# Result stores of two batches in their own stream, wider idle matmuls, a stacked short tile, and another order

## The chip, the core and the metric

The kernel runs on one core of a Trainium2 chip. A core has a matrix engine (PE, with its weight loads PEld), three engines for elementwise work (DVE, ACT and POOL) and SP, which only issues DMA transfers, in order. All engines take their instructions in program order and wait for each other through semaphores. The metric is the device time of one execution in microseconds (us); lower is better.

## The reference

The inputs are q, k and v (8 batches, 8 heads, 576 positions, 64 channels a head) and four weights. For each batch:

```
q_d, k_d, v_d = means over groups of 4 positions (576 -> 144)
pooled        = repeat(softmax(q_d k_d^T / 8) v_d, 4)
local         = softmax over |i - j| < 4 of (q k^T / 8), times v
x             = pooled + local, as [576, 512]
u             = x + (relu(x^T w_tok1) w_tok2)^T       # tokens: 576 -> 256 -> 576
out           = u + relu(u w_ch1) w_ch2               # channels: 512 -> 1536 -> 512
```

## The kernel before

Everything is written by one Python function that places instructions by hand. Each piece of work is a generator that yields steps (engine, planned duration, what must have been made, PSUM or SBUF slots taken and given back) and emits its instructions after each step. `drive` simulates clocks for all engines and always emits the step that can begin first; steps within `PATIENCE` of the first, on the same engine, go by the order of the list of streams, which for the first part of the kernel is the string `PRIORITY` (one letter for a group of streams). So the planned durations and that string set the order of every engine's instructions, and of the DMAs in SP's queue; on the chip only semaphores and program order count.

- *Attention, batch by batch.* `load` fetches q and k (tile qk), `load_v` fetches v in pieces (vr) which POOL adds to the pooled values vd, `load_w` fetches v in the order of the local windows (vw). `pooled` makes the scores sd of a pair of heads (PE), their exponentials pd, the transposed td, the product ad, and od (DVE, L551); after the last pair two DMAs copy od into rows of vw (L557). `local` makes the scores sc of a tile of 128 positions (the fifth tile has 64), masks, softmax (DVE and ACT, tile P), the transposed pT and the product av, which takes the pooled result along with vw; ACT copies it to x. The local products of a batch thus wait for vw and for od's copy.
- *Exponentials.* In batches listed in `BIASED` the maximum goes into four ACT activations as a bias (L515, reading PSUM); in the others DVE subtracts it (L521) and ACT runs one activation (L524).
- *Token mix (`mix`).* Batch 0 uses float32 weights. From batch 1 on, weights and x are split in a high and a low part (`token_split`; `splits`: xh, ACT copies, DVE subtracts) and `mm3` runs three passes over them, `PASSES` = high by high, high by low, low by high. u is the sum; its maximum scales it to two float16 parts, uh.
- *Channel mix.* Batches 0 and 1 run plain products: `first` (12 tiles by uh and the weight C1, matmuls c, L128) and `second` (by C2); `second_up` adds the result to u (L891) and issues the store (L892) in the same step. Batches 2 to 7 run a product scheme with fewer multiplications, from sums of the weights that POOL and DVE make meanwhile (`weight_sums`, stored to DRAM by `stores`, L912 and L916, and fetched as units, L1010); `first_blocks` (L1029) and `second_blocks` (L1197) are its products, `after_second` adds to u, and `results` stores.
- *Weights.* They arrive as 64-bit words. `weight_loads` (L241) fetches W (token weights, nine pieces), C1 (twelve pieces of 512 KB) and `C2.loads` (L379) the twelve of C2; ACT, POOL and DVE turn each into float32 (`to_f32`, L220, L223, L225). `in_turn` makes each of these transfers wait for the third one before it (`DEPTH`), and SP with it.
- *Idle matmuls.* Until batch 0's uh is planned, `keep_busy` (L170) fills planned gaps of PE with products of a constant tile.

The first batches' work overlaps: batch 1's attention and mix lie between batch 0's channel products, batch 2's between batch 1's.

## Time and profile before

| | |
|---|---|
| median of 3 runs | 894.14 us (891.07 to 894.2) |
| profiled execution | 896.11 us, its span 894.0 us |
| mean granted PE clock | 0.981 |
| busy | PE 95%, PEld 77%, DVE 71%, ACT 47%, POOL 44% |
| DMA | 152.85 MB, mean 171 GB/s |

The span runs from the first to the last instruction. An engine's busy time is that of its instructions; matmuls are pipelined and their ends are modelled, so a busy PE can be slower than its peak, and the granted clock tells how fast it was allowed to run. Where a line names a releaser ("<-"), the instruction waited for that one last.

### The profile page before, as it was taken

How to read it: one execution, taken by the hardware profiler on the slowest of the kernel's cores; microseconds unless marked ns; L12 is line 12 of the kernel's file. 1: busy time of each engine (PE TensorE's matmuls, PEld its weight loads, DVE VectorE, ACT ScalarE, POOL GpSimd, SP SyncE). 2: the span in 40 equal slices, each digit the busy share in tenths (PEclk: the TensorE clock that was granted, in tenths of full speed). 3: DMA queues.
4: the chain of work that ended last, by engine and by line, in shares of the span. 5: the costliest groups of instructions: out<-in, count | busy, mean ns of one | idle time of the engine just before them, and what ended most of it. 6: DMA issues, size and time to landing. Idle time of an engine off the chain costs nothing.

```text
span 894.0 us, 26687 instructions
## 1 busy us (share of the span) xinstructions
PE 850.5 (95%) x11112; PEld 685.4 (77%) x11112; DVE 636.2 (71%) x1410; ACT 420.2 (47%) x978; POOL 392.4 (44%) x593
## 2 busy tenths in 40 slices
PE   7699999897999999999999999999999999999998
PEld 6566777686779877888868887888768886887776
DVE  6669998568886756868585876678485885666762
ACT  2366552134553335754365525654265535643740
POOL 6228475769496203662066403761066501420430
PEclk9798999898999999999999999999999999999999
DMA  8775524663264308636673557545574554247653
GB/s 267 262 270 188 163 64 138 221 210 91 87 230 116 92 26 292 219 111 174 192 243 135 161 184 247 200 135 172 171 241 146 154 192 133 95 125 211 196 162 121
DMA packets 71656, 152.85 MB, mean 171 GB/s; under 512 B 16560, under 2 KB 32432, under 8 KB 69488
## 3 DMA queue, kind: packets, MB, share of 16 engines
q1 hardware_dynamic: 71536, 151.16, 52.1%
q8 instruction: 87, 1.43, 0.6%
q14 instruction: 33, 0.27, 0.1%
HBM read 128.32 MB, written 20.45 MB: 166 GB/s over the span
## 4 chain that ended last, share of the span: by engine, by line
PE 81%; DVE 9%; DMA 4%; POOL 2%; ACT 2%; issue 2%; SPq 1%; ACTq 0%; DVEq 0%; POOLq 0%
PE dX L1197 12%; PE c L128 12%; PE t L128 11%; PE cx L1029 11%; PE dY L1197 6%; PE cy L1029 5%; PE ad L541 3%; PE dZ L1197 3%; PE cz L1029 3%; PE av L619 3%; PE sc L577 2%; PE sd L503 2%; PE pT L605 2%; PE td L531 2%; PE t L690 2%
## 5 line engine op out<-in xcount | busy, mean ns | idle before, releaser
L1109 POOL TENSOR_TENSOR h<-t,h 128x288 f16<-128x288 f32 x108 | 82.6, 768 | 213.4 <-ACT h L1098 211.6
L1029 PEld LDWEIGHTS <-wa 128*128 128x128 f16 x864 | 82.0, 98 | 26.7 <-issue 4.7
L1197 PEld LDWEIGHTS <-wc_S 128*128 128x128 f16 x864 | 82.8, 98 | 21.4 <-issue 1.3
L1029 PEld LDWEIGHTS <-wb 128*128 128x128 f16 x648 | 62.6, 98 | 19.6 <-issue 4.1
L128 PE MATMUL c<-uh,CW 128*128 128x288 f16 x576 | 76.7, 289 | 0.0
L128 PE MATMUL c<-h,CX 128*128 128x288 f16 x576 | 76.2, 290 | 0.1
L1197 PEld LDWEIGHTS <-wc_A 128*128 128x128 f16 x648 | 62.7, 98 | 15.5 <-issue 0.2
L128 PEld LDWEIGHTS <-CX 128*128 128x128 f16 x576 | 55.6, 99 | 15.8 <-issue 0.8
L128 PEld LDWEIGHTS <-CW 128*128 128x128 f16 x576 | 55.7, 99 | 14.7 <-issue 0.6
L1029 PE MATMUL cx<-uh_T,wb 128*128 128x288 f16 x432 | 64.7, 286 | 1.3 <-DVE y L1140 1.3
L128 PE MATMUL t<-xh,W 128*128 128x512 f32 x210 | 58.9, 414 | 7.1 <-DVE xh L660 5.0
L487 POOL TENSOR_TENSOR qd<-qk 128x144 f32<-128x144 f32 x48 | 28.8, 599 | 83.9 <-DMA qk<-in_qk_dram 83.9
L487 POOL TENSOR_TENSOR qd<-qd,qk 128x144 f32<-128x144 f32 x96 | 61.7, 642 | 6.3
L457 POOL TENSOR_TENSOR vr<-vr 72x256 f32<-72x256 f32 x48 | 36.4, 759 | 58.5 <-DMA vr<-in_vr_dram 51.2
L1197 PE MATMUL dY<-h,wc_S 128*128 128x288 f16 x432 | 58.4, 286 | 0.0
L128 PE MATMUL t<-W,hid 128*128 128x288 f32 x336 | 58.4, 309 | 0.0
L1197 PE MATMUL dX<-h,wc_S 128*128 128x288 f16 x432 | 58.2, 286 | 0.0
L1197 PE MATMUL dX<-h,wc_A 128*128 128x288 f16 x432 | 57.0, 286 | 0.0
L1098 ACT ACTIVATE h<-t 128x288 f16<-128x288 f32 x108 | 47.7, 442 | 15.6 <-DVE t L1113 15.5
L128 PEld LDWEIGHTS t<-xh,W 128*128 128x128 f32 x210 | 37.1, 188 | 17.6 <-DVE xh L660 7.6
L1244 DVE SCALAR_TENSOR_TENSOR u<-dX,io,u 128x288 f32<-128x288 f32 x48 | 24.7, 515 | 34.3 <-PE dX L1197 33.7
L128 PEld LDWEIGHTS t<-W,hid 128*128 128x128 f32 x336 | 46.6, 189 | 0.0
(206 smaller groups left out, 1946.7 us busy)
## 6 DMA issues: line engine op xcount, KB each, us to landing
qk<-in_qk_dram SPq DMA_DIRECT2D x32, 580.0 KB
wa<-d1a SPq DMA_DIRECT2D x36, 512.0 KB
wc_S<-d_S SPq DMA_DIRECT2D x48, 384.0 KB
wb<-d1b SPq DMA_DIRECT2D x36, 384.0 KB
wc_A<-d_A SPq DMA_DIRECT2D x36, 384.0 KB
vw<-in_vw_dram SPq DMA_DIRECT2D x8, 1280.0 KB
vr<-in_vr_dram SPq DMA_DIRECT2D x64, 144.0 KB
vw<-in_vw_dram SPq DMA_DIRECT2D x8, 1024.0 KB
```

The source lines that it names most:

```text
L128: nc.tensor.matmul(ps, lhs(a), rhs(c), start=first and i == 0, stop=last and i == 2, **kw)
L457: nc.gpsimd.tensor_add(t[:, 0:2], t[:, 0:2], t[:, 2:4])
L487: nc.gpsimd.tensor_add(to, to if f > 1 else x[0], x[f])
L503: nc.tensor.matmul(ps[:G, par, Sd * g:Sd * g + Sd], st.qd[p, pr, 0, G * g:G * g + G], st.qd[p, pr, 1], start=True, stop=True)
L531: nc.tensor.transpose(ps[:G, par, o:o + G], pd[:, par, g, G * kg:G * kg + G], ident[:G, :G])
L541: nc.tensor.matmul(ps[:, g, par], pt[:, par, kg, G * g:G * g + G], st.vd[:, kg, 2 * pr + par], start=kg == 0, stop=kg == 1)
L619: nc.tensor.matmul(ps[QB * j:QB * j + QB, par, D * hp:D * hp + D], pt[p, hp, QB * j:QB * j + QB], st.vw[p, g, h, D * hp:D * hp + D], start ...
L1029: nc.tensor.matmul(ps, w[:, a, 128 * k:128 * k + 128], uh[x][:, k, c], start=first_ and k == j == 0, stop=k == 1 and j == 2, skip_group_ch ...
L1098: nc.scalar.activation(here().h[:, PARTS.index(name), 0], x, f)
L1109: nc.gpsimd.tensor_tensor(h[:, i, 1], getattr(here(), x), h[:, i, 0], ALU.subtract)
L1197: nc.tensor.matmul(ps, w[:, k, a], H[k][:, i, c], start=first_ and k == j == 0, stop=k == 5 and j == 2, skip_group_check=True)
L1244: nc.vector.scalar_tensor_tensor(u, blocks_[b, o, name], io, u, ALU.mult, ALU.add)
```

## The change

- The eight result stores of batch 0, and those of batch 1, leave `second_up`; a stream of their own (`plain_results`) issues each in a step on SP, planned no earlier than `LATE` = 14 us after its data. Those of batches 2 to 6 are planned 3 us after theirs.
- `in_turn` counts bytes: a transfer waits until it and those under way before it are at most 1.2 MB.
- An idle matmul has 384 columns (the 192 read twice) instead of 192, and there are half as many for each unit of planned gap; 0.85 of a gap is filled instead of 0.6, at most 12 units instead of 8.
- The token mix's fifth tile has only 64 rows. The weight's other 64 rows now hold its low part, and x's high part is copied to both halves, so that two passes (`STACKED`) do what three did. ACT copies twice instead of once.
- `BIASED` takes in batches 0 and 1; in batch 0 the last multiply of the local softmax (L600) moves from DVE to POOL.
- vr of batch 0 lies in buffers of u instead of x, xh and od.
- Planned durations, first clocks, `PATIENCE`, `HELD`, a factor 1.04 on DVE's steps, and the string `PRIORITY` differ, so the order of instructions differs on all engines.

```diff
@@ -23,18 +23,21 @@
...
 PASSES = ((0, 0), (0, 1), (1, 0))
+STACKED = ((0, 0), (1, 1))
 FIRSTS = (0, 1, 4, 5, 8, 9)
...
 LIVE = 3
-PATIENCE = 0.15
+PATIENCE = 0.1
 GATE = (0, 0, 1, 2, 3)
-BIASED = range(2, 8)
+BIASED = range(0, 8)
 ON_POOL = range(2, 8)
+LATE = 14.0
 HOP = 0.12
-HELD = 0.6
+HELD = 0.8
+MARGIN = 1.04
 TURN = 0.1
-DEPTH = 3
-PRIORITY = "LpWUMASETaCDPHmQw"
+UNDER_WAY = 1.2e6
+PRIORITY = "SUMWpTaCEADPLHmQw"
@@ -123,9 +126,9 @@
...
-    def mm3(ps, lhs, rhs, first, last, **kw):
-        for i, (a, c) in enumerate(PASSES):
-            nc.tensor.matmul(ps, lhs(a), rhs(c), start=first and i == 0, stop=last and i == 2, **kw)
+    def mm3(ps, lhs, rhs, first, last, passes=PASSES, **kw):
+        for i, (a, c) in enumerate(passes):
+            nc.tensor.matmul(ps, lhs(a), rhs(c), start=first and i == 0, stop=last and i == len(passes) - 1, **kw)
@@ -138,14 +141,14 @@
...
-    clock = dict(A=2.0, G=5.0, V=2.0, P=0.0, S=0.0, D=0.0, R=0.0, X=0.0)
+    clock = dict(A=2.0, G=5.0, V=2.0, P=6.6, S=0.0, D=1.5, R=0.0, X=0.0)
     now = [0.0]
...
     def step(engine, us, *needs, at=None, take="", give="", mode=None, port=False):
-        return engine, us, needs, at, take.split(), give.split(), mode, port or engine == "G"
+        return engine, us * MARGIN if engine == "V" else us, needs, at, take.split(), give.split(), mode, port or engine == "G"
@@ -166,8 +169,9 @@
...
             ps = P1("busy")
-            for _ in range(8 * n // 3):
-                nc.tensor.matmul(ps[:, :192], junk[:, :128], junk, start=True, stop=True)
+            wide = junk.unsqueeze(1).to_broadcast([128, 2, 192])
+            for _ in range(4 * n // 3):
+                nc.tensor.matmul(ps[:, :384].rearrange("p (k n) -> p k n", k=2), junk[:, :128], wide, start=True, stop=True)
@@ -191,7 +195,7 @@
...
                 if ("uh", 0, 1) not in made and free["g"]:
-                    keep_busy(min(8, int((t - clock["P"]) * 0.6 / 0.22)))
+                    keep_busy(min(12, int((t - clock["P"]) * 0.85 / 0.22)))
                 mode = m
@@ -216,29 +220,33 @@
...
         lo, hi = words[:, :, 0], words[:, :, 1]
-        yield step("A", 0.1 + n * 0.0011, at=at)
+        yield step("A", 0.28 + n * 0.00077, at=at)
         nc.scalar.activation(hi.bitcast(F32), hi.bitcast(F32), AF.Prelu, scale=2.0 ** -112, alpha=-2.0 ** 32)
-        yield step("G", 0.1 + n * 0.0016)
+        yield step("G", 0.09 + n * 0.0013)
...
         nc.gpsimd.tensor_scalar(lo, lo, 2.0 ** -29, -0.501, ALU.mult, ALU.add)
-        e = yield step("V", 0.08 + n * 0.0012, *needs, port=True)
+        e = yield step("V", 0.1 + n * 0.0014, *needs, port=True)
         nc.vector.scalar_tensor_tensor(lo if y is None else y(), hi, 3, lo, ALU.logical_shift_left, ALU.bitwise_or)
...
-    def in_turn(dma):
-        if len(queue) >= DEPTH:
-            tc.add_manual_dep(dma.ins, queue[-DEPTH].ins.name, mybir.DependencyInfo(mybir.DependencyClass.Sync, mybir.DependencyReason.DATA),
-                              reason="few transfers under way")
-        queue.append(dma)
+    def in_turn(dma, nbytes):
+        before, n = len(queue), nbytes
+        while before and n + queue[before - 1][1] <= UNDER_WAY:
+            before -= 1
+            n += queue[before][1]
+        if before:
+            tc.add_manual_dep(dma.ins, queue[before - 1][0].ins.name, mybir.DependencyInfo(mybir.DependencyClass.Sync, mybir.DependencyReason.DATA),
+                              reason="few bytes under way")
+        queue.append((dma, nbytes))
...
             raws[i] = T([src.shape[0], 2 * n], U32, tag, f"{name}{i}_raw")
-            in_turn(nc.sync.dma_start(raws[i], src))
+            in_turn(nc.sync.dma_start(raws[i], src), src.shape[0] * n * 8)
             made[name, "raw", i] = fetched(src.shape[0] * n * 8, n * 0.7e3)
@@ -256,8 +264,10 @@
...
         nc.scalar.copy(f[:, 0], WY[i])
+        if f.shape[0] == short:
+            nc.scalar.copy(f[:, 1], WY[i])
         e = yield step("V", 0.08 + n * 0.0012, port=True)
-        nc.vector.tensor_tensor(f[:, 1], WY[i], f[:, 0].bitcast(F32), ALU.subtract)
+        nc.vector.tensor_tensor(W1[-1][short:, 0] if f.shape[0] == short else f[:, 1], WY[i], f[:, 0].bitcast(F32), ALU.subtract)
         make(("W", "split", i), e)
@@ -309,7 +319,7 @@
...
             nc.scalar.activation(f[:, 0], y, AF.Copy, scale=self.s[i // 4])
-            t = yield step("V", 0.75, port=True)
+            t = yield step("V", 0.88, port=True)
             nc.vector.scalar_tensor_tensor(f[:, 1], y, self.s[i // 4], f[:, 0], ALU.mult, ALU.subtract)
@@ -376,7 +386,7 @@
...
                     t = four[:, i % 4]
-                in_turn(nc.sync.dma_start(t, u32(c2[i])))
+                in_turn(nc.sync.dma_start(t, u32(c2[i])), 2 ** 19)
                 self.raws.append(t)
@@ -420,8 +430,7 @@
...
-            tag = "x" if st.b or i < 4 else "xh" if i < 7 else "od"
-            ts[i] = T([G, 4, 128], F32, tag, f"vr{st.b}_{i}")
+            ts[i] = T([G, 4, 128], F32, "x" if st.b else "u", f"vr{st.b}_{i}")
             nc.sync.dma_start(ts[i], vr[st.b, g, pr].rearrange("p (r c) -> p r c", r=4))
@@ -474,7 +483,7 @@
...
             for h in range(2):
-                yield step("V", 0.44, at=0.0 if h else st.at[hp])
+                yield step("V", 0.5, at=0.0 if h else st.at[hp])
                 o = st.qd[:, hp, 0, G * h:G * h + G].rearrange("p (r g) -> p r g", g=HG)
@@ -522,7 +531,7 @@
...
             nc.scalar.activation(pd, pd, AF.Exp, scale=0.125 / 16)
-        yield step("P", 0.55 if b < 2 else 0.46, take="gg", give="w")
+        yield step("P", 0.5 if b < 2 else 0.46, take="gg", give="w")
         ps = P2(f"td{b}_{pr}")
@@ -532,7 +541,7 @@
...
         nc.scalar.copy(pt, ps[:G, :, :2 * Sd].rearrange("p a (k w) -> p a k w", k=2))
-        yield step("P", 1.2 if b < 2 else 0.97, ("v", b, 2 * pr), ("v", b, 2 * pr + 1), *([("full", b - 1)] if b and pr == 0 else []),
+        yield step("P", 1.1 if b < 2 else 0.97, ("v", b, 2 * pr), ("v", b, 2 * pr + 1), *([("full", b - 1)] if b and pr == 0 else []),
                    *([("od", b)] if pr else []), take=one, give="w")
@@ -596,8 +605,8 @@
...
         nc.vector.reciprocal(r, r)
-        yield step("V", 0.5, at=0.0, port=True)
-        nc.vector.tensor_tensor(w, w, r.unsqueeze(2).unsqueeze(2).to_broadcast([n, H, 8, 5]), ALU.mult)
+        yield step("G" if b < 1 else "V", 0.9 if b < 1 else 0.5, at=None if b < 1 else 0.0, port=True)
+        (nc.gpsimd if b < 1 else nc.vector).tensor_tensor(w, w, r.unsqueeze(2).unsqueeze(2).to_broadcast([n, H, 8, 5]), ALU.mult)
         before = [("av", b, t - 2)] if t > 1 else [("av", b - 1, 3 + t)] if b else []
@@ -652,17 +661,21 @@
...
             for t in range(NT if b else 0):
-                yield step("A", 0.62, ("x", b, t), *([("over", 0, 0)] if b == 1 else []),
+                yield step("A", 0.62 if t < NT - 1 else 1.2, ("x", b, t), *([("over", 0, 0)] if b == 1 else []),
                            *([("t1", b, t - 3)] if t > 2 else [("mixed", b - 1)] if b > 1 else []))
                 xh = st.xh[t] = T([128, 2, 512], F32R, "xh", f"xh{b}_{t}")
-                nc.scalar.copy(xh[:, 0], xf(t))
+                if t < NT - 1:
+                    nc.scalar.copy(xh[:, 0], xf(t))
+                else:
+                    for p in (0, short):
+                        nc.scalar.copy(xh[p:p + short, 0], xf(t)[:short])
                 e = yield step("V", 0.7, port=True)
...
             for t in range(NT):
-                e = yield step("P", 1.8 if b == 0 else 1.5 if b == 1 else 1.42, *([("W", "split", t), ("xh", b, t)] if b else [("W", "y", t), ("x", 0, t)]),
+                e = yield step("P", 1.8 if b == 0 else (1.5 if b == 1 else 1.42) * (1 if t < NT - 1 else 2 / 3), *([("W", "split", t), ("xh", b, t)] if b else [("W", "y", t), ("x", 0, t)]),
                                take="" if t else f"gg>{b}")
@@ -673,7 +686,7 @@
...
                         mm3(st.acc[:, f], lambda a: W1[t][:, a, 128 * f:128 * f + 128], lambda a: st.xh[t][:, a],
-                            t == 0, t == NT - 1)
+                            t == 0, t == NT - 1, PASSES if t < NT - 1 else STACKED)
                 make(("t1", b, t), e)
@@ -889,8 +902,15 @@
...
             nc.vector.scalar_tensor_tensor(us[c], banks[c], io, us[c], ALU.mult, ALU.add)
-            nc.sync.dma_start(out[b, 128 * c:128 * c + 128, s0:s0 + N], us[c])
+            make(("into", b, ch, c), e, LATE)
         make(("over", b, ch), e)
+
+    def plain_results(b):
+        for ch in range(2):
+            for c in range(4):
+                yield step("S", 0.1, ("into", b, ch, c))
+                nc.sync.dma_start(out[b, 128 * c:128 * c + 128, HALF * ch:HALF * ch + HALF], ready[b].u[ch][c])
+                fetched(147e3, 250e3)
@@ -1222,7 +1242,7 @@
...
             for name, h in (("A12", 0), ("A22", 1)):
-                yield step("S", 0.1, ("into", b, o, name))
+                yield step("S", 0.1, ("out", b, o, name))
                 c = o + 2 * h
@@ -1243,6 +1263,7 @@
...
                 make(("into", b, o, name), e)
+                make(("out", b, o, name), e, 3.0 if b < B - 1 else 0.0)
@@ -1315,7 +1336,7 @@
...
         group["Q"] = products[2:]
-        streams = [reopen()] + [x for k in PRIORITY for x in group[k]]
+        streams = [reopen(), plain_results(0), plain_results(1)] + [x for k in PRIORITY for x in group[k]]
         late = []
```

## The prediction

> **What bounds the kernel now.** I read the page's head first, then busy time by stage, then the chain of waits in the weakest stages, then the DMA queue there.
>
> ```profile
> span 894.0 us, 26687 instructions
> PE 850.5 (95%) x11112; PEld 685.4 (77%) x11112; DVE 636.2 (71%) x1410; ACT 420.2 (47%) x978; POOL 392.4 (44%) x593
> ```
>
> The span is PE's: 43.5 us idle in all. Stages, in stretches of 20 us or more, and the bad places in 5 us (columns: span, then busy time of PE, PEld, DVE, ACT, POOL with instruction counts, granted clock, DMA share, GB/s):
>
> ```profile
> 140.00:160.00 20.00, 18.42 (x259) 14.98 (x258) 17.35 (x44) 5.43 (x10) 15.16 (x21) 1.00 0.59 212
> 400.00:500.00 100.00, 98.02 (x1274) 79.73 (x1272) 71.98 (x159) 51.42 (x125) 41.89 (x65) 1.00 0.59 187
> 600.00:700.00 100.00, 96.56 (x1237) 78.80 (x1236) 71.69 (x158) 52.09 (x126) 39.67 (x62) 1.00 0.56 183
> ...
> 165.00:170.00 5.00, 2.43 (x20) 1.70 (x18) 1.44 (x3) 0.42 (x1) 4.53 (x9) 1.00 0.69 231
> 170.00:175.00 5.00, 3.33 (x134) 2.90 (x135) 2.56 (x3) 1.91 (x4) 4.70 (x8) 0.65 0.15 49
> 175.00:180.00 5.00, 5.00 (x84) 3.50 (x83) 1.72 (x3) 2.45 (x6) 0.23 (x1) 0.66 0.33 78
> 205.00:210.00 5.00, 2.87 (x30) 2.11 (x29) 4.90 (x10) 0.96 (x2) 4.43 (x7) 1.00 0.13 39
> 210.00:215.00 5.00, 2.36 (x22) 2.17 (x23) 3.35 (x9) 4.03 (x12) 4.60 (x7) 0.75 0.48 125
> 215.00:220.00 5.00, 5.00 (x155) 4.17 (x154) 3.01 (x8) 1.00 (x3) 4.62 (x7) 0.57 0.31 82
> ```
>
> From 400 us on PE is 96 to 98% busy, so a microsecond that batches 0 and 1 give back earlier reaches the end whole: what runs there is PE work that waits for little but PE. Earlier, two holes matter: 165 to 175 (4.2 us idle) and 205 to 215 (4.8 us), and behind each of them PE runs cold: (3.33+5.00)x0.35 = 2.9 us lost at clock 0.65, and 2.36x0.25+5.00x0.43 = 2.7 us at 0.75 and 0.57. Together 14.6 us. The chain says where the first comes from (start, duration, what):
>
> ```profile
> 137.09 0.53 DVE u L891
> 137.63 0.37 SPq L892
> 138.11 2.50 DMA vr<-in_vr_dram
> ...
> 153.20 0.53 DVE u L891
> 154.18 0.61 SPq L466
> 154.84 11.42 DMA vw<-in_vw_dram
> 166.70 0.73 SPq L557
> 167.48 3.35 DMA vw<-od
> 170.87 1.81 PE av L619 x111
> ```
>
> Twice the chain leaves a result (u, L891) for a load of batch 1 that has nothing to do with it: the store (L892) stands in SP's queue ahead of vr (values to be pooled) and of vw (attention's values), and SP issues in order. SP's waits from 116 to 182 us and POOL's from 100 on (total, times, longest), and three instructions of DVE and PE that date what follows:
>
> ```profile
> SPq L892 <- DVE u L891: 18.0, 2, 16.3
> SPq L912 <- DVE S L955: 7.8, 2, 6.8
> ...
> POOL vr L439 <- DMA vr<-in_vr_dram: 10.5, 2, 10.2
> ...
> 113.91 1.48 DVE L225 SCALAR_TENSOR_TENSOR CY<-C_raws 128x512 uint32<-128x512 uint32 x1
> 156.10 0.42 DVE L551 TENSOR_TENSOR od<-ad,rd 72x256 f32<-72x256 f32 x1
> 213.73 0.61 DVE L764 SCALAR_TENSOR_TENSOR uh<-u,us,uh 128x288 f16<-128x288 f32 x1 [0.98 <-ACT uh L762]
> ...
> 205.09 1.64 PE L128 MATMUL c<-h,CX 128*128 128x288 f16 x12
> ```
>
> SP stood 16.3 us (to 137.6) with vr behind the store, and POOL stood idle 10.2 us for that vr. The last pooled result of batch 1 (od) is ready at 156.5, but its copy into vw (L557) goes out at 166.70, when vw itself has landed. Batch 0's last product ends at 206.7, batch 1's first input (uh) is ready at 214.3: the second hole.
>
> **The change, part by part.**
>
> *Stores of batches 0 and 1 in a stream of their own, planned 14 us after their data.* Same eight DMAs for each batch, moved behind later loads in SP's queue. vw may load once C2's raws are read (the last CY conversion ends at 115.4), so it is issued near 121, where the store began to block, instead of 154 and lands in 11.4 us (its row), by 133. The copy of od then waits for od alone: 157 instead of 166.7, and PE's av starts at about 160 instead of 170.1; earlier still if vr, no longer behind the store, lets POOL finish vd ten microseconds sooner. The first hole goes whole, 4.2+2.9 = 7.1. In the second PE is out of work. Batch 1's mix starts 10 us earlier, but batch 0's products also end 7 us earlier, so I give back only half: 3.8 of 4.8+2.7. Late next there: DVE, which gives batch 1's attention and its splits. Sum of this part **-10.9**; bounds -14.6 and 0. A store that is late holds a u buffer, but batch 2 takes batch 0's and batch 3 batch 1's only with the results of their own mix, which stand well over 14 us behind the last use. Cost 0; if it were wrong, up to 14 once for each.
>
> By the Trainium skill ("TensorE: Matmul & The Clock Gate", the section on HAM oscillation) the clock falls to half after idle gaps of more than about 3.4 us. The trace departs from it here: 3.33 us of work in the five from 170, and 2.43 in the five before, were followed by 0.66 with PE fully busy. Were the 2.9 us not this hole's, the sum would come out at 883 instead of 880; I go by the rows.
>
> *Stacked short tile.* In batches 1 to 7 the last tile of the first token product goes from three passes to two: 2 matmuls of 128x512 fewer for each batch. Price by the chain, where they stand back to back, and what is added:
>
> ```profile
> 340.31 2.79 PE t L128 x12
> ...
> L658 ACT CAST xh<-x_last x7: 602/607/622, 184.6 to 767.6; 128x512 fp32r<-128x512 f32 x7
> ...
> PE t L128 <- DVE xh L660: 4.6, 4, 1.9
> ```
>
> 0.2325 each, x14 = **-3.3**. Added: a second ACT copy of 0.61 us ahead of the same tile's split, seven times. ACT is 47% busy over the span, but PE already waits for splits, 4.6 us from 400 on; if each of the seven came late by the whole copy it would cost 4.3. The planner counts the copy (1.2 for 0.62) and puts PE's tile behind other products, so I take 0 and keep +4.3 as a bound.
>
> *Idle matmuls.* Half as many of twice the columns: about the same time for each unit, but planned for 0.85 of a gap instead of 0.6, at most 12 units instead of 8.
>
> ```profile
> 44.88 5.52 PE t L672 x8
> 54.07 3.63 PE t L672 x8
> ```
>
> The same eight products of batch 0's token mix run cold the first time, 5.52 against 3.63, behind the wait for od's copy that the next part shows: 1.9 us to be had if the filler bridged it. But the planner, which places the filler, does not see that wait. A filler that overruns costs at most its extra length, a fourth more than now on some 2 us. Taken 0; +1 to -1.9.
>
> *Bytes instead of transfers under way (1.2 MB for three).* For W four go at once; for C1 and C2 (524 KB) two instead of three. SP's queue in the first 40 us, the pooled result, and how C1's second half landed:
>
> ```profile
> 32.38 5.66 SPq L241 DMA_DIRECT2D W_raw<-in_w_dram  x4
> 38.09 1.53 SPq L557 DMA_DIRECT2D vw<-od  x2
> 32.66 0.42 DVE L551 TENSOR_TENSOR od<-ad,rd 72x256 f32<-72x256 f32 x1
> ...
> 47.04 4.01 SPq L241 DMA_DIRECT2D C_raw<-in_c_dram  x4
> 50.82 0.65 POOL L223 TENSOR_SCALAR C_raw<-C_raw 128x512 uint32<-128x512 uint32 x1 [8.58 <-DMA C_raw<-in_c_dram]
> 54.32 0.78 POOL L223 TENSOR_SCALAR C_raw<-C_raw 128x512 uint32<-128x512 uint32 x1 [0.27 <-DMA C_raw<-in_c_dram]
> ```
>
> Batch 0's od is ready at 33.1 and waits 5 us behind four W loads, each held by the rule of three. Under the new rule the last of them waits for the last C1 load and not for the first W of the four: about 1 us earlier; 5 if the new order puts od's copy ahead. Against it: C1's first lands after 3.8 us (47.0 to 50.8), the third at 54.3, so one every 1.75 us with three under way; a load's round trip is then 3x1.75 = 5.3 us. Two under way make one every 1.9 us if the round trip falls back to 3.8, and every 2.6 if it stays: an estimate from these rows, 0.15 to 0.9 us later for each of C1's twelve loads, whose sums are on the way to the first product. I take the lower end, since the loads queue behind each other now; it about cancels the 1 us: **0**, from -5 to +10.5.
>
> *Bias in the activation for batches 0 and 1, and one multiply of batch 0 on POOL.*
>
> ```profile
> L521 DVE TENSOR_TENSOR pd<-sd,mxd x16: 443/448/454, 11.6 to 143.3; 72x288 f32<-72x288 f32 x16
> L515 ACT ACTIVATE pd<-sd,mxd x96: 361/372/382, 210.6 to 715.2; 72x144 f32<-72x144 f32 x96
> ```
>
> DVE loses 16x0.448 = 7.2 us and gains 8 scalings of four columns; ACT issues 32 activations of 0.372, 11.9 us, where it issued 8 of four times the columns, hidden by its 53% idle; POOL, 44% busy, takes five multiplies of about the size of L521's, which DVE is rid of. In batch 0 the pooled result comes 2 to 3 us sooner, but is held by the W loads above; in batch 1 it is part of what lets av start at 160. Counted there; by itself 0, to -3.
>
> *The rest.* Stores of batches 2 to 6 three microseconds later: 0. What stands behind them in SP's queue are weight loads that PE does not wait for in the rows above. vr of batch 0 in u buffers: both it and the first u come before any of them is wanted twice, 0. Planner durations, margin, held share, patience, first clocks and the priority string alter the order everywhere: no row prices that. The nearest is how two like stretches differ, 98.0 against 96.6 busy: 1.5 us in 100. Taken 0; six stretches make -6 to +9.
>
> Sum: 10.9+3.3 = 14.2. The profiled execution took 896.1 (2.1 around its span), 2.0 above the median of 894.1; the terms are differences, so I set them against the median: **880**. Own range of this case 872 to 888.
>
> **The rivals.**
> - *Little of the holes closes:* batch 1's attention is DVE's (17.35 of 20 busy at 140 to 160), so mix 1 comes hardly earlier and the second hole grows by what the first gives. For: that DVE row. Against: DVE is busy only 5.7 of the 15 us from 165 on. With a fourth of the 14.6: 894.1-3.3-3.6 = 887.
> - *The change doesn't do what it says:* something else holds vw's load in SP's queue; stores of weight sums (L912) wait there too. Then 894.1-3.3 = 891. Against: their two waits on DVE took 7.8 us, the result stores' two 18.0.
> - *Slower:* the limit of two 512 KB loads decides. If each of C1's twelve loads takes the upper end, 2.6 us, the first product slips 10.5 us, and with no hole closed 894.1+10.5-3.3 = 901. It decides from about 0.65 us for each load on (7.8-3.3 = 0.5%). For: POOL waits for C1 as quoted. Against: C1's second half is also held by its buffers.
> - *More:* od of batch 0 goes out when ready (-5), its cold products go (-1.9) and most of the second hole too (-2.5): 871.
>
> **How the numbers follow.** Half a per cent is 4.5 us, about what a measurement can tell here: faster is below 889.6, slower above 898.6. Chances: forecast 0.50, first rival 0.17, no effect 0.11, slower 0.11, more 0.11. Faster: 0.50+0.11+0.15 = 0.76; same 0.13 (no effect, and the rest of the first); slower 0.11. Range 866 to 896: it leaves out the slower half of the slow rival and the best of the last, beyond what is counted.
>
> **What the profile after would show.** Right: no SP wait of L892 longer than a few microseconds, vw's load of batch 1 near 121, av of batch 1 by 162, no 5 us stretch between 150 and 225 below 4 us of PE at a clock under 0.9; 196 matmuls of t on xh instead of 210. Wrong: vw's load still after 140; PE's hole moved to 190 to 205 with DVE full; C1's conversions waiting for C_raw at once for longer than 8.6 us; new idle of PE after 300.

## The result and the profile after

The changed kernel took 901.87 us (median of 6 runs, 900.32 to 906.04), the kernel before 893.78 (6 runs): a ratio of 1.0108 with the interval [1.0085, 1.0132]. It is slower by about 1%, where 880 us, faster by 1.6%, was forecast, and outside the range of 866 to 896. The profiled execution took 901.76 us. Its page's head:

```profile
span 899.9 us, 26563 instructions
PE 852.0 (95%) x11055; PEld 676.6 (75%) x11055; DVE 622.8 (69%) x1396; ACT 429.3 (48%) x1010; POOL 403.1 (45%) x599
```

TensorE issues 57 instructions fewer and is as busy as before (852.0 for 850.5 us); it stands idle for 47.9 us instead of 43.5. Busy time by stretch, the same stretches and columns as in the prediction, and two more ahead of batch 1's av:

```profile
140.00:160.00 20.00, 17.88 (x249) 14.36 (x246) 18.86 (x45) 6.43 (x15) 8.16 (x12) 1.00 0.40 130
400.00:500.00 100.00, 97.61 (x1334) 79.26 (x1332) 70.26 (x163) 52.85 (x128) 43.59 (x66) 1.00 0.56 187
600.00:700.00 100.00, 97.56 (x1335) 79.47 (x1336) 71.09 (x161) 52.86 (x127) 42.55 (x65) 1.00 0.55 184
158.09:163.09 5.00, 0.68 (x5) 0.17 (x2) 2.28 (x5) 0.00 (x0) 4.61 (x8) 0.80 0.78 275
163.09:168.09 5.00, 4.95 (x140) 3.94 (x141) 0.84 (x2) 2.07 (x4) 4.53 (x10) 0.52 0.03 7
165.00:170.00 5.00, 5.00 (x99) 3.67 (x87) 2.17 (x3) 2.02 (x4) 4.53 (x9) 0.71 0.18 59
170.00:175.00 5.00, 5.00 (x125) 3.81 (x124) 3.92 (x7) 3.40 (x9) 2.92 (x5) 1.00 0.09 30
205.00:210.00 5.00, 4.33 (x42) 3.27 (x41) 4.38 (x9) 2.46 (x6) 4.10 (x7) 1.00 0.17 53
210.00:215.00 5.00, 1.93 (x13) 1.58 (x14) 4.56 (x11) 3.17 (x11) 4.75 (x5) 0.73 0.53 136
215.00:220.00 5.00, 5.00 (x148) 3.94 (x146) 1.93 (x7) 1.39 (x4) 4.55 (x8) 0.59 0.38 116
```

The hole at 165 to 175 is not closed: it came forward with av, to 158 to 163 (0.68 us of work in five), and the clock falls behind it as before (0.80, then 0.52). The hole at 205 to 215 with its cold clock (0.73, 0.59) is as it was. TensorE's longest waits from 95 to 240 us (total, times, longest), first the kernel before, then the changed one:

```profile
PE td L531 <- ACT pd L515: 4.8, 2, 4.0
PE av L619 <- DMA vw<-od: 4.1, 3, 2.7
```

```profile
PE av L628 <- DMA vw<-od: 4.4, 2, 4.1
PE td L540 <- DVE mxd L519: 3.7, 1, 3.7
```

The first hole is av's wait for the copy of od, the second the wait of td for batch 2's exponentials pd, and both are there about as long as before. SyncE's issues around batch 1's attention, its waits from 116 to 182 us (total, times, longest), and the chain:

```profile
130.35 0.82 SPq L475 DMA_DIRECT2D vw<-in_vw_dram  x2
...
150.78 2.09 SPq L420 DMA_DIRECT2D qk<-in_qk_dram  x4
...
153.84 1.62 SPq L566 DMA_DIRECT2D vw<-od  x2
```

```profile
SPq L420 <- PE sc L586: 13.7, 1, 13.7
...
SPq L912 <- DMA qk<-in_qk_dram: 2.3, 1, 2.3
```

```profile
147.44 0.42 DVE od L560
...
154.49 0.24 SPq L566
154.78 8.32 DMA vw<-od
163.14 2.04 PE av L628 x119
```

The stores (now L912) no longer hold SyncE until VectorE is done: their longest wait is 2.3 us, where two of them had waited 18.0. The load of v of batch 1 goes out at 130.35 for 154.18, av starts at 162.5 for 170.1. But the copy of od, ready at 147.9, is issued at 153.84, behind the loads of q and k of batch 2 (L420), which waited 13.7 us for TensorE to be done with their buffers, and then it takes 8.32 us where it took 3.35: 2.3 MB were put into the queue just ahead of it.

Four stretches tell of every run where its time lies: up to the first C1 product (A), from there to the first product of batch 2 (B), to the first of batch 7 (C), and the rest (D). Starts and ends are those of single instructions in the traces. The labels are those of the experiments below.

| kernel | A | B | C | D | ratio [95%] |
|---|---|---|---|---|---|
| before | 83.1 | 252.1 | 491.3 | 67.4 | 1 |
| after | 83.1 | 253.5 | 492.3 | 71.0 | 1.0108 [1.0085, 1.0132] |
| e1 old edits, new order | 78.7 | 253.9 | 493.1 | 71.0 | 1.0070 [1.0043, 1.0096] |
| e2 new edits, old order | 89.9 | 250.6 | 484.8 | 67.4 | 1.0039 [1.0013, 1.0066] |
| e3 short tile only | 84.6 | 251.5 | 487.8 | 67.4 | 0.9952 [0.9924, 0.9980] |
| e4 stores only | 83.0 | 255.2 | 493.9 | 67.4 | 1.0023 [0.9997, 1.0048] |
| e5 byte limit only | 88.8 | 252.5 | 489.8 | 67.4 | 1.0076 [1.0045, 1.0108] |
| e6 after, three transfers | 81.7 | 252.4 | 491.6 | 71.0 | 1.0061 [1.0036, 1.0087] |
| e7 old order, new from batch 2 | 80.0 | 250.7 | 493.5 | 71.0 | 1.0062 [1.0039, 1.0084] |
| e8 after, old last batch | 82.1 | 258.1 | 491.3 | 67.4 | 1.0045 [1.0019, 1.0071] |
| e9 wide idle matmuls only | 84.0 | 251.3 | 487.5 | 67.4 | 0.9966 [0.9945, 0.9988] |
| e10 after, q and k behind copy | 86.6 | 246.9 | 492.0 | 71.0 | 1.0063 [1.0036, 1.0089] |
| e11 after, three, old from batch 2 | 84.8 | 252.5 | 485.3 | 67.4 | 0.9966 [0.9941, 0.9991] |
| e12 short tile, four transfers | 79.7 | 251.2 | 490.3 | 67.4 | 0.9935 [0.9913, 0.9957] |
| e13 after again | 84.7 | 253.7 | 493.9 | 71.0 | 1.0122 [1.0101, 1.0143] |
| e14 v load alone first | 80.6 | 250.0 | 494.5 | 67.4 | 0.9999 [0.9980, 1.0018] |
| e15 after, mended | 80.3 | 246.8 | 485.8 | 67.4 | 0.9845 [0.9816, 0.9874] |
| e16 short tile, wide idle, four | 79.8 | 251.1 | 488.2 | 67.4 | 0.9921 [0.9895, 0.9947] |
| e17 mended, no stream | 78.4 | 250.7 | 487.6 | 67.6 | 0.9903 [0.9870, 0.9935] |
| e18 mended, byte limit | 81.1 | 249.7 | 485.3 | 68.2 | 0.9920 [0.9887, 0.9953] |

A stretch is one execution. Runs that share the instructions of a stretch give its scatter: A is 80.0 to 84.6 in the five kernels with the old order, the old edits there and three transfers (before, e3, e4, e7, e9); D repeats to a tenth. B is 250.7 to 252.5 in four kernels with the instructions of the kernel before there (before, e5, e7, e9) and 253.5 to 258.1 in three with those of the changed one (after, e8, e13); C is 487.5 to 491.3 in three with the same instructions there (before, e5, e9). A difference of a few microseconds between two traces proves nothing there. A ratio is that of all runs against the kernel before on the same chip (median there 893.8 to 895.4).

### The profile page after: what moved, and what is told of

The parts are those of the page before. It is cut to its first block, busy times and chain, and to the rows that moved or that the text cites. A ratio compares the mean times of both kernels' runs of the same rounds, so it can differ in the third digit from the quotient of the medians.

```text
span 899.9 us, 26563 instructions
## 1 busy us (share of the span) xinstructions
PE 852.0 (95%) x11055; PEld 676.6 (75%) x11055; DVE 622.8 (69%) x1396; ACT 429.3 (48%) x1010; POOL 403.1 (45%) x599
## 4 chain that ended last, share of the span: by engine, by line
PE 85%; DVE 8%; ACT 3%; DMA 2%; issue 2%; SPq 0%; ACTq 0%; DVEq 0%
PE c L131 13%; PE dX L1217 12%; PE t L131 11%; PE cx L1049 11%; PE dY L1217 6%; PE cy L1049 5%; PE ad L550 4%; PE dZ L1217 3%; PE sc L586 3%; PE cz L1049 3%; PE av L628 3%; DMA vw<-od 2%; PE sd L512 2%; PE td L540 2%; PE pT L614 2%; PE busy L174 2%
## 5 line engine op out<-in xcount | busy, mean ns | idle before, releaser
L1129 POOL TENSOR_TENSOR h<-t,h 128x288 f16<-128x288 f32 x108 | 87.6, 813 | 203.7 <-ACT h L1118 200.6
L1049 PE MATMUL cx<-uh_T,wb 128*128 128x288 f16 x432 | 64.8, 286 | 1.8 <-DVE y L1160 1.8
L496 POOL TENSOR_TENSOR qd<-qd,qk 128x144 f32<-128x144 f32 x96 | 58.2, 606 | 6.1
L131 PE MATMUL t<-xh,W 128*128 128x512 f32 x196 | 56.7, 417 | 3.9 <-DVE xh L673 2.9
L524 ACT ACTIVATE pd<-sd,mxd 72x144 f32<-72x144 f32 x128 | 37.7, 373 | 28.8 <-DVE mxd L519 16.8
```

What stands on the lines that cost most here:

```text
L131: nc.tensor.matmul(ps, lhs(a), rhs(c), start=first and i == 0, stop=last and i == len(passes) - 1, **kw)
L496: nc.gpsimd.tensor_add(to, to if f > 1 else x[0], x[f])
L524: nc.scalar.activation(pd[:, par, g], s[:, par, g], AF.Exp, bias=mx[:, par, g:g + 1], scale=0.125 / 16)
L1049: nc.tensor.matmul(ps, w[:, a, 128 * k:128 * k + 128], uh[x][:, k, c], start=first_ and k == j == 0, stop=k == 1 and j == 2, skip_group_ch ...
L1129: nc.gpsimd.tensor_tensor(h[:, i, 1], getattr(here(), x), h[:, i, 0], ALU.subtract)
```

## The experiments

In all of them the order of the steps is written out: the planner's picks were recorded for the kernel before and for the changed one and are replayed, so that an edit moves little or nothing else. "Old" and "new" order are these two lists. The whole change is thus an edit list and an order.

**Edits and order apart.** e1 is the kernel before in the new order, e2 the changed kernel in the old one (stores by the planner's times), e3 and e4 one edit each in the old order.

```diff
 e3  -  passes=((0,0),(0,1),(1,0))
     +  passes=PASSES if t < NT - 1 else ((0,0),(1,1))    # and the second copy of the short tile
 e4  -  nc.sync.dma_start(out[b, ...], us[c])             # behind the last VectorE step of batches 0, 1
     +  make(("into", b, ch, c), e, LATE)                 # issued by plain_results(b)
```

> All computations, transfers and limits of the kernel before, but its steps issued in the recorded order of the changed kernel (no edit of the change is in it, only the order that its planner chose; a store of batch 0 or 1 goes out with its result). Theory ORDER (the order on the engines is what made it slower, the edits by themselves gain): as slow as the changed kernel or some 3 us slower, since the short tile has three passes again, 902 to 908 us (ratio 1.010 to 1.016). Rival EDITS (limits, idle matmuls, doubled copy, late stores cost): close to the kernel before, 890 to 896 (0.996 to 1.003).

> All edits of the change, but the steps issued in the recorded order of the kernel before; only the stores of batches 0 and 1 are put in by the plan, 14 us after their data. Theory ORDER: faster than before by the short tile at least, 884 to 891 us (0.990 to 0.997). Rival EDITS: slow like the changed kernel, 898 to 904 (1.005 to 1.012).

> The kernel before in its own order, with one edit: the short tile stacked, two passes for three and a second ACT copy. My step of the prediction: -3.3 us, 890 to 891 (0.9963). Rival (the doubled copy makes its split late, 0.6 us for each of seven batches): +1, 894 to 895 (1.001).

> The kernel before in its own order, with one edit: the stores of batches 0 and 1 in their own stream, 14 us late in the plan. My step of the prediction: -10.9 us, 883 (0.988), with vw of batch 1 issued near 121. Rival (vw stands behind other work in SP's queue, first of all qk of batch 2, which waits for PE's scores of batch 1 to 150): vw goes out at 152, av at 168 instead of 170, -1 to -3, 891 to 893 (0.997 to 0.999). vr goes out by 125 in both.

Measured: 900.33, 898.87, 891.06 and 896.37 us. The order alone loses 0.7%, the edits alone 0.4%, though the short tile in them gains 0.5%; so neither of the two theories of e1 and e2 holds by itself, and the two losses add up to that of the changed kernel. The stream of stores alone, the largest term of the forecast, gains nothing; e4 came out above its rival's range too. e4's waits of SyncE from 116 to 182 us and its chain say why:

```profile
SPq L477 <- PE sc L644: 16.3, 1, 16.3
...
SPq L624 <- DMA vw<-in_vw_dram: 2.6, 1, 2.6
```

```profile
154.46 0.37 SPq L477
...
157.68 0.45 SPq L533
158.18 11.31 DMA vw<-in_vw_dram
```

The 16.3 us that SyncE had stood behind a store, it now stands behind the loads of q and k of batch 2 (L477), the next in the list ahead of the load of v (L533), which goes out at 157.68 instead of 154.18. In e1, without the stream, the new order has the load of v ahead of both: issued at 125.3, av 79.6 us behind the first C1 product, as in the changed kernel (79.4), and od is ready 64.7 us behind it, in the changed kernel 64.8 (73.5 in the kernel before). So what the changed kernel did gain at av came from the order.

**The byte limit.** e5 is the kernel before with it, e6 the changed kernel without it.

```diff
 e5  -  if len(queue) >= 3: wait for queue[-3]
     +  wait for the last transfer that 1.2e6 bytes under way leave out
 e6  the reverse, in the changed kernel
```

> The kernel before, every instruction in its own recorded order, with one edit: the limit on loads under way counts bytes (1.2e6) and no longer three transfers. Theory (the byte limit is what costs the changed edits their time in the first 90 us): the conversion of the weights of the first channel product waits for its half-MB loads, that product starts 4 to 7 us later than 83.07 us, its first 25 products end later too, and the time is 898 to 901 us, a ratio of 1.004 to 1.007. Rival (the loss comes from the wider idle matmuls or from the bias moved to ScalarE in batches 0 and 1): the product starts within 1 us of 83 us and the ratio is 0.998 to 1.001.

> The changed kernel, every instruction in its own recorded order, with the old limit of three transfers under way in place of the bytes. Theory of the byte limit: 4 us come back at the first channel product of batch 0 (79 us for 83.09), and the time is 896 to 899 us, against 901.9 of the changed kernel, a ratio of 1.002 to 1.006. Rival (the limit costs nothing): 1.009 to 1.012.

Measured: 902.11 and 900.24 us. The first C1 product starts at 88.8 us in e5, and at 89.9 in e2, against 80.0 to 84.6. Busy time in the stretches in which C1's second half and C2 are loaded, first the kernel before, then e5 (the last two columns are DMA share and GB/s):

```profile
48.00:56.00 8.00, 7.53 (x154) 4.68 (x153) 5.15 (x11) 4.75 (x11) 2.88 (x4) 0.96 0.94 325
56.00:64.00 8.00, 8.00 (x80) 4.93 (x80) 5.72 (x14) 5.69 (x11) 2.61 (x4) 1.00 0.91 320
64.00:72.00 8.00, 7.81 (x53) 6.11 (x52) 6.57 (x11) 6.74 (x14) 4.04 (x4) 1.00 0.96 305
```

```profile
48.00:56.00 8.00, 7.55 (x155) 4.75 (x154) 5.77 (x11) 5.19 (x12) 2.62 (x3) 1.00 0.84 268
56.00:64.00 8.00, 7.49 (x76) 4.47 (x75) 4.27 (x12) 4.83 (x10) 2.53 (x4) 1.00 0.78 225
64.00:72.00 8.00, 7.81 (x54) 6.20 (x52) 6.54 (x9) 5.57 (x12) 3.65 (x5) 1.00 0.81 246
```

Two half-MB loads under way leave the DMA engines a fifth idle, and move 225 to 268 GB/s for 305 to 325. The cost, 5.8 us in A, is 0.48 us for each of C1's twelve loads (by the scatter of A, 0.35 to 0.73). The last two of them are issued at 63.37 us instead of 59.46. In the changed kernel the traces place only a part of it: A is 81.7 in e6 and 82.1 to 86.6 in four with the limit (after, e8, e10, e13).

**The new order behind batch 2.** e7 is the kernel before with the old order up to there and the new one behind; e8 the changed kernel with six VectorE and two ScalarE instructions of the last batch in the old order:

```diff
 e8, VectorE, in four rounds of the last batch (two more pairs change places in the first and last round)
 -  s <- cz, s          (waits for cz)
    h <- cx, h          (lower half of h; frees the buffer of cx)
 +  s <- cz, s
```

> All edits left out; only the order: the old one up to the first product of batch 2 (335 us), the new one from there. With the new order throughout the time was 900.3 (ratio 1.007). Theory (the new order loses behind batch 2, in the last batch, 4.5 us of waits of TensorE against 1.3, and about 2.6 us in batches 5 to 7): 899 to 901 us, ratio 1.005 to 1.008. Rival (only the last batch's waits are the order's doing, the rest of its loss lies ahead of 335 us): 896.5 to 898, ratio 1.003 to 1.004.

> The changed kernel with its order but for the last batch, where six VectorE instructions and two of ScalarE stand as in the old order: the lower half of h is split off (h from cx) ahead of the addition that waits for cz. Theory: the four waits of 0.91 us of TensorE for that split, and the one of 0.9 us, go, the one of 1.3 us of the kernel before comes in their place, and the time falls by 3.2 us, to 898.5 us (ratio 1.005 to 1.009). Rival (the buffer is late for another reason, the wait then names another releaser): no change, ratio 1.009 to 1.012.

Measured: 900.73 and 899.51 us. e7 loses as much as the new order throughout. TensorE's waits in the last batch, the changed kernel and then e8:

```profile
PE cx L1049 <- DVE h L1122: 3.6, 4, 0.9
PE cx L1049 <- DVE y L1160: 0.9, 1, 0.9
```

```profile
PE cx L1114 <- DVE y L1225: 1.3, 1, 1.3
```

D falls from 71.0 to 67.4 us, as the theory had it: the addition that waited for cz held back the instruction that frees the buffer of cx. In batches 2 to 6 the new order has the like on ScalarE; three lines of the changed kernel's timeline:

```profile
448.36 0.91 PE L1049 MATMUL cy<-uh_T,wa 128*128 128x288 f16 x6
...
452.06 0.38 ACT L1157 COPY y<-cy 128x288 f32<-128x288 f32 x1
...
452.49 0.90 PE L1049 MATMUL cy<-uh_B,wa 128*128 128x288 f16 x6 [1.75 <-ACT y L1157]
```

The copy of cy stands behind other activations for nearly 3 us, and the next cy waits; four times, 6.6 us from 345 to 810 us, where the kernel before has no such wait. That this list is the cause is not tested by itself as in the last batch; with the old order from batch 2 on (e11, e15) these waits are gone.

**Idle matmuls, the place of the copy, sums of parts.** e9 is the kernel before with the wide idle matmuls; e10 the changed kernel with one more condition on the loads of q and k; e11 the changed kernel with three transfers, and the old order from batch 2 on; e12 is e3 with four transfers.

```diff
 e9   -  8 * n // 3 matmuls of 192 columns, up to 8, for 0.6 of the gap
      +  4 * n // 3 matmuls of 384 columns, up to 12, for 0.85 of the gap
 e10  -  yield step("S", 0.1, *(("sc", b - 1, t) for t in every))
      +  yield step("S", 0.1, *(("sc", b - 1, t) for t in every), *([("full", 1)] if b == 2 else []))
 e12  -  DEPTH = 3
      +  DEPTH = 4
```

> The kernel before in its own recorded order with one edit: half as many idle matmuls of 384 columns in place of 192, and the new count of them. Theory (they fill waits that end with something else): 893 to 897 us, ratio 0.998 to 1.002. Rival (a cold array takes the wide ones longer, so that real products queue behind them, and this is a part of what the changed edits lose in the first 90 us): the first channel product starts 2 us or more later than in the other runs with the old edits (80.0 to 84.6 us), ratio 1.003 or more.

> The changed kernel in its own order but for one step: the four 580 KB loads of q and k of batch 2 are issued behind the copy of od of batch 1, not just ahead of it (six rows of SyncE's list change place, two of POOL's, none of TensorE's, VectorE's or ScalarE's). Theory A (the gain of the earlier load of v was lost to contention: the copy took 8.32 us for 3.35): the copy takes 3 to 4 us, the av products of batch 1 start near 158 us for 162.5, and 4 us of it reach batch 2: ratio 1.003 to 1.007. Theory B (VectorE, 95% busy from 90 to 160 us, sets how much TensorE idles ahead of batch 2, and a hole closed opens another): the copy is as short and av as early, but the first product of batch 2 and the time stay: ratio 1.007 to 1.012.

> The changed kernel with the two parts that the runs found to lose taken out: three transfers for the bytes, and the old order from the first product of batch 2 on. What is left of the change is the stream of stores, the stacked short tile, the idle matmuls, the bias of batches 0 and 1, and the new order ahead of batch 2. If the parts add up: 1.0061 (with three transfers) less 0.0062 (the new order behind batch 2) is 1.000, 893 to 898 us. If the new order ahead of batch 2 is worth something by itself: below 0.9952, the short tile's ratio alone, 890 us or less.

> The kernel before in its own order with the stacked short tile, and four transfers under way in place of three. The limit of 1.2e6 bytes lets two half-MB loads be under way, and cost 0.0076; with three the DMA engines were 0.91 to 0.96 busy from 48 to 72 us. Theory (three fill them): the short tile's ratio, 0.993 to 0.997. Rival (each further transfer still shortens the loads): the first channel product 3 us or more earlier than the 80.0 to 84.6 us of the runs with three, and a ratio of 0.992 or less.

Measured: 891.25, 899.29, 890.25 and 887.43 us. e9 was timed 0.3% faster, but its trace has the gain in C (487.5), where no idle matmul runs and the instructions are those of before, and not in A or B; so this is no proof for the idle matmuls. e10's issues of SyncE:

```profile
149.88 1.46 SPq L631 DMA_DIRECT2D vw<-od  x2
152.77 1.94 SPq L485 DMA_DIRECT2D qk<-in_qk_dram  x4
```

TensorE no longer waits for the copy at all; av starts 73.7 us behind the first C1 product for 79.4, and B is 246.9 us for 253.5: theory A holds, and the gain stays. e11 comes out 0.34% better than the sum, at 0.9966. The new order may take the short tile's gain behind batch 2: with the tile C is 484.8 to 490.3 in the old order (eight traces) and 491.3 to 493.9 in the new one (five), without it 487.5 to 491.3 (before, e5, e9) and 493.1 and 493.5 (e1, e7). By these spreads that is possible and not shown. e12: the fourth transfer gave 79.7 us in A and a ratio of 0.9935 for 0.9952; in its first stretch from 48 us the DMA engines moved more than with three, so three had not filled them, against the theory:

```profile
48.00:56.00 8.00, 7.61 (x181) 4.56 (x159) 5.17 (x8) 6.92 (x16) 3.79 (x5) 1.00 1.01 405
```

In time the gain of the fourth transfer is not certain: the two intervals overlap, and the ratio lies in the range of the theory.

**The changed kernel on the same chip, the load of v alone, a mended kernel.** e13 is the changed kernel once more; e14 is e4 with the stores and the loads of q and k held back behind the copy of od (the condition of e10 on both); e15 is the changed kernel with e10's edit, four transfers, and the old order from batch 2 on; e16 is e12 with e9's idle matmuls.

> The changed kernel with its own recorded order written out (six rows of SyncE's list differ), as the measure for the others of this call. Theory: 1.008 to 1.012, and with it three transfers (1.0061) and the loads of q and k behind the copy (1.0063) each were worth 0.2 to 0.5%. Rival: 1.005 to 1.007, and neither was worth anything in this order.

> The kernel before in its own order, with the stores of batches 0 and 1 in a stream of their own, and both these stores and the loads of q and k of batch 2 held back behind the copy of od of batch 1, so that on SyncE nothing that waits stands ahead of the load of v of batch 1. With the stores alone moved, SyncE waited 16.3 us at the loads of q and k instead, and the load of v went out at 157.7 us. Theory (the step of the prediction failed for that one wait only): the load of v goes out by 130 us, the copy near 162 or earlier, av of batch 1 starts at 160 to 164 us for 172.4, the first product of batch 2 comes 5 to 8 us earlier, ratio 0.990 to 0.996. Rival (VectorE is 95% busy there and the idle time of TensorE only moves): av as early, the first product of batch 2 within 2 us of 335 to 338, ratio 0.999 to 1.003.

> The changed kernel with four transfers under way in place of the bytes, the loads of q and k of batch 2 behind the copy of od, and the old order from batch 2 on. With three transfers and the old order from batch 2 on the ratio was 0.9966; the copy is worth 0.002 to 0.005 by what the changed kernel gave, the fourth transfer 0.001 to 0.002: 0.990 to 0.994, 885 to 889 us. If the gain of the copy is taken up by waits elsewhere: 0.995 to 0.998.

> The kernel before in its own order with the stacked short tile, four transfers and the wide idle matmuls. Short tile and four transfers gave 0.9935, the wide idle matmuls alone 0.9966: if these add up 0.990, 885 us; if the gain of the idle matmuls was chance, 0.993 to 0.995.

Measured: 905.11, 894.66, 879.78 and 886.87 us. Against e13's 1.0122, three transfers (e6, 1.0061) and the copy ahead of q and k (e10, 1.0063) are worth 0.6% each (0.45 to 0.47% against the changed kernel's first ratio, 1.0108). e16's 0.9921 is within the error of e12's 0.9935, so the idle matmuls add nothing certain. e14 missed: with two obstacles gone, the load of v went out at 135.9 us and the copy at 160.4 only. Its waits of SyncE from 116 to 182 us:

```profile
SPq L986 <- DVE SV_sum L1054: 16.9, 1, 16.9
```

and two of TensorE's from 95 to 240 us, which the kernel before does not have:

```profile
PE c L185 <- DVE CX L379: 2.5, 3, 1.5
PE t L756 <- DVE umx L811: 1.8, 1, 1.8
```

A store of weight sums (L986) is the third in the old list that waits for 16 us in front of the copy, after the result store and the loads of q and k. So e14 does not decide whether VectorE would have set B with the copy early. But it speaks for the rival: TensorE's waits for the copy fell from 4.1 to 0.6 us, these two for VectorE came in their place, and the ratio of 0.9999 is in the rival's range. In the new order a part of the gain stays: with the copy early B is 246.9, 246.8 and 249.7 (e10, e15 and, below, e18), for 253.5 and more in the changed kernel. e15, the fastest kernel of all, is 0.9845 [0.9816, 0.9874], half a per cent below the least that was expected (0.990), and what gave that is not shown. 97% of its span is on TensorE:

```profile
span 880.4 us, 26582 instructions
PE 849.8 (97%) x11055; PEld 675.8 (77%) x11055; DVE 620.9 (71%) x1396; ACT 427.0 (48%) x1010; POOL 399.6 (45%) x599
```

```profile
400.00:500.00 100.00, 99.77 (x1352) 80.94 (x1349) 71.68 (x167) 53.41 (x129) 43.41 (x67) 1.00 0.58 189
600.00:700.00 100.00, 99.74 (x1354) 81.15 (x1352) 71.87 (x168) 54.15 (x133) 42.01 (x66) 1.00 0.57 187
...
155.34:160.34 5.00, 3.53 (x145) 2.81 (x143) 3.94 (x8) 2.08 (x4) 4.69 (x7) 1.00 0.52 168
160.34:165.34 5.00, 4.88 (x155) 3.79 (x155) 2.23 (x5) 2.63 (x6) 4.53 (x10) 1.00 0.20 65
200.34:205.34 5.00, 1.48 (x21) 1.04 (x18) 4.93 (x10) 1.36 (x6) 4.66 (x6) 1.00 0.32 78
...
205.78:210.78 5.00, 5.00 (x141) 4.01 (x141) 3.57 (x9) 2.90 (x8) 4.55 (x8) 0.66 0.34 91
```

```profile
PE td L601 <- ACT pd L585: 6.0, 2, 3.5
```

The first hole is down to 1.6 us, and the clock stays at 1.00 behind it. The second hole is not closed; it came forward to 200 to 205 (3.5 us idle, then 0.66): TensorE waits for batch 2's exponentials, and VectorE, which makes their maxima, is busy 4.93 of the five microseconds. Behind 400 us TensorE is 99.7% busy.

**What single parts are worth in the mended kernel.**

```diff
 e17  +  nc.sync.dma_start(out[b, ...], us[c])             # e15 without the stream of stores
 e18  -  DEPTH = 4                                         # e15 with the byte limit
      +  UNDER_WAY = 1.2e6
```

> The mended kernel (0.9845) with the stores of batches 0 and 1 back where the kernel before issues them, behind their last VectorE step; all else as in it. In the new order the load of v of batch 1 stands ahead of all these stores. Theory (the stream of stores by itself is worth nothing in the new order): ratio 0.982 to 0.988, av of batch 1 75 to 77 us behind the first channel product, as with the stream (75.3). Rival (two stores that wait for VectorE ahead of the copy of od hold it up, and the stream is a part of the gain): the copy issued 3 us or more later, ratio 0.989 or more.

> The mended kernel (0.9845) with the limit of 1.2e6 bytes in place of four transfers. Theory (two half-MB loads under way do not fill the DMA engines, in this order too): the first channel product starts 2 to 6 us later than 80.34 us, ratio 0.989 to 0.992. Rival (in the new order the loads start early enough): 0.983 to 0.987.

Measured: 885.92 and 885.98 us. Against e15 the stream is worth 0.58% (1 - 0.9845/0.9903); the two intervals just touch (0.9874 and 0.9870), so it is a gain of uncertain size, and e17 lies in the rival's range. In e17 two stores stand ahead of the copy, which is issued 68.9 us behind the first C1 product for 64.9; av is not later, the 3.9 us lie in B behind it; but e18, with the stream, has 249.7 there, near e17's 250.7. So how the stream gains is not shown. The byte limit costs 0.75% here too; A is only 0.7 us longer, but the 25th C1 product starts 8.0 us behind the first for 5.3.

## Why the prediction was wrong, step by step

- *Stores, -10.9: failed, in two steps.* The wait was read rightly, and it went. The first failed step is "so it is issued near 121, where the store began to block". Behind the store the old list had two more that waited as long, q and k for sc (16.3 us in e4) and the weight sums (16.9 in e14), so that the part alone gave 1.0023. The second is "The first hole goes whole". In the changed kernel the new order had the load of v ahead of the stores anyway (e1); it went out at 130 and av began at 162.5, near the forecast's 160. But the hole came along, since the copy of od stood behind q and k (8.32 us for 3.35): TensorE waited 4.4 us for it, for 4.1 before, and B is 253.5 for 252.1. With the list put right (e15) that hole is down to 1.6 us and B is 246.8. The half of the second hole (3.8) never came: what ended it was not batch 1's uh, as the prediction read it, but pd of batch 2, behind a full VectorE, 4.0 us before and 3.5 in e15. "Late next there: DVE" was right, but the forecast gave half of that hole back all the same. The second rival had said that something else holds vw's load in SyncE's queue; the stores of weight sums that it named come only third, after q and k. The first, that little of the holes closes and the idle time moves, fits e14.
- *Byte limit, 0: mis-sized.* Its rows gave 0.15 to 0.9 us for each load and I took the lower end, "since the loads queue behind each other now"; 0.48 was measured, 5.8 us in A and 6.8 in the ratio of e5 (1.0076). That is the slow rival's mechanism, at half its price; with no hole closed it made up most of the loss. The sign named for it, one conversion that waits longer than 8.6 us, did not come (7.6 in e5): the delay builds up from load to load.
- *The rest, 0: mis-sized.* The order behind batch 2 costs 0.62% (e7), 5.5 us, within the +9 that stood as its bound. The sign named, new idle time of TensorE after 300 us, is there: 3.6 us at h in the last batch and 6.6 us at y; the waits for xh fell in turn, from 7.0 to 3.8 us.
- *Short tile, -3.3: right.* 0.9952, -4.3 us [-6.8, -1.8]; the second copy was not late (the waits for xh behind 345 us are 6.1 us in e3, 7.0 before). In the new order little of it shows: the changed kernel without the byte limit (e6, 1.0061) is only 0.1% below e1 (1.0070), which has none of the edits. Why is open.
- *Idle matmuls, 0:* not contradicted; e9's -0.34% does not lie where they run. *Bias and the multiply on POOL, 0:* not run alone, and open; batch 1's od is no sooner with them (64.8 us behind the first C1 product) than in e1 without (64.7). What e2 (1.0039) leaves after the byte limit (0.0076), short tile (-0.0048) and stores (0.0023) is -0.0012, within the errors.
- *The sum.* e15 comes out at 880, but that is the forecast's number for another kernel: it has neither the byte limit nor the new order behind batch 2, and moves the copy, which the forecast did not see. That the two agree is luck.

## What to carry to other kernels

On a queue that issues in order, a wait that is taken away is worth only the distance to the next instruction that waits: list all that stand ahead of the load that matters, with what each waits for, before giving the hole back. A hole that is no longer at its old time may only have moved: look for the wait that made it, not for the stretch. The same holds within an engine's list: an instruction that frees a buffer must not stand behind one that waits for a later product. A new order of a tuned schedule is a change of its own and needs its own term; recorded and replayed apart from the edits, it can be priced.

## What the hardware showed

- Half-MB loads: two under way moved 225 to 268 GB/s from 48 to 72 us (e5, e2), three 288 to 358 (six traces with the old list), four 405 and 412 from 48 to 56 us and 336 and 356 in the next eight (e12, e16). A DMA share of 0.94 with three was not yet the limit: with four it was 1.01 and 1.03.
- A copy of 288 KB took 8.32 us when 2.3 MB had been issued on its queue 3 us before, and 3.35 us in the kernel before, where these loads had gone out 17 us ahead of it.
- The clock fell behind a wait of 3.74 us of the changed kernel (0.73 and 0.59 from 210 us on), as behind its 4.11 us ahead of av (0.52 from 163 us on):

```profile
213.07 1.18 PE L540 MATMUL td<-ident,pd 72*72 72x72 f32 x8 [3.74 <-DVE mxd L519]
```

  The Trainium skill ("TensorE: Matmul & The Clock Gate", the section on HAM oscillation) has the clock halved after idle gaps of more than about 3.4 us; this place agrees, the kernel before's 0.65 at 170 us, told of in the prediction, does not: its longest wait there was 2.66 us, in 3.45 us that held only 0.27 us of work.
- Kernels with the same instructions up to the first C1 product started it between 80.0 and 84.6 us; differences of a few microseconds there between two single traces say nothing.
